# A new written-out order for a fused attention and gated linear unit: other engines for copies, V products and masks, other PSUM banks and buffers

## The chip, the cores and the metric

One core of one Trainium2 chip runs the whole program. The metric is the device time of one execution in microseconds, as the median of several runs. TensorE is called PE in the profile's rows (its weight loads PEld), VectorE DVE, ScalarE ACT, GpSimd POOL and SyncE SP; DMAs here are issued from SP's queue, and two at the start from ACT's.

## The reference, cut to what matters

Eight batches, eight heads, 576 positions, head size 64. A causal attention has a decay bias that depends on running sums of `s`; its output, 512 wide, goes through a gated unit: a causal convolution of 5 taps and a sigmoid make the gate, a matrix product makes the value, a second matrix product the output.

```python
scores = scale * np.matmul(q, k.transpose(0, 1, 3, 2))
cum = np.cumsum(np.maximum(s, 0.0), axis=-1)
bias = -(cum[:, :, :, None] - cum[:, :, None, :])
scores = np.where(causal, -1000000000.0, scores + np.minimum(bias, 0.0))
attn = softmax(scores);  x = heads side by side of np.matmul(attn, v)
gate = 1.0 / (1.0 + np.exp(-sum_k conv_w[k] * shifted(x, 4 - k)))
out = (gate * (x @ w_val)) @ w_out
```

## The kernel before, in words

The work is cut into *pairs*: pair n is two heads of batch n // 4 and also the 128-wide slice n % 4 of that batch's 512 columns. There are 32 of them. The order of all work on all engines is one table of words in the source, `ORDER`. A word such as `vp.1.0:G` or `av0.4:T:6+7` gives a step, its indices, its engine (S SyncE, G GpSimd, T TensorE, A ScalarE, V VectorE) and, after the second colon, the PSUM banks or the buffer that it uses. The program walks the table once and issues each word's instructions on its engine. Each engine then runs its own instructions in that order, and waits by semaphores for what it reads or overwrites. The table is the change; the functions behind the words are the same (line numbers after the change are 3 to 4 lower).

The steps, with the line that the profile shows for them:

- `ld_q`, `ld_k`, `ld_t`, `ld_v`, `ld_s`, `ld_cw`, `ld_wv`, `ld_wo` load (L434, L439, L462, L471, L472, L475 and others), `st` stores (L737); all but two of them stand in SP's queue.
- `c_q`, `c_k` cast queries and keys to bf16 (L377, `qkb<-first`, `qkb<-qkf`); `qt` (batch 0) and `qq` (later batches) transpose them on TensorE (L492, L632); `qe` copies the result from PSUM to `QKT` (L377), for later batches as 512 int32 words, each of which holds two bf16. `tt` and `te` do the same for the last 64 positions (L484).
- `s0`, `s1`, `s2` are the score products of a pair (L508), `e0`, `e1`, `e2` their exponentials into `P` (ScalarE, L559, 1024 columns each). `s4`, `e4` (L535) are the last 64 positions of a batch's four pairs. For pairs 28 to 31 the halves `u0` to `u3` and `f0` to `f3` (L573) take their place.
- The causal mask has two forms. Where the table has a word `mk.n` (or `ml.n`, for the second half of a split pair), GpSimd overwrites with zeros the entries of `P` above the diagonal (L582). Where it has none, two more products on TensorE (`future`, L521) add a large negative number to the scores ahead of the exponential. So a word that is left out of the table puts its mask on TensorE.
- `vp.b.p` is the V product: values of batch b, two heads, times the decay of their key, `Vp <- vst, w` (L478, 128x650, both inputs in SBUF). `av0`, `av` multiply `P` with it (L597), `rec` and `nm` normalise (L610, L616, into `xn`), `xt` transposes (L629), `xe` copies to `xT` (L377; bf16 on VectorE, int32 on ScalarE).
- `t1` is the first two taps of the convolution (VectorE, L671); each of the taps 2 to 4 is either one VectorE instruction that reads PSUM (`t2` to `t4`, L676), or a product `p2` to `p4` into `pr` (GpSimd L660, ScalarE L658) and a sum on GpSimd (L679).
- `th` is the gate's tanh (ScalarE, L696), `val` the value product (L709), `glu` gate times value (VectorE, L718), `out` the output product (L729), `oe` its copy to `ot` (L377).
- `wu` is an unread product: 512 columns of the identity times itself on TensorE, written to a bank and never read (L623).

```python
on_pool = {(f, int(n[0])) for f, *n in (name.split(".") for name, *_ in steps) if f in ("mk", "ml")}
for name, e, *slots in steps:
    ...
    does[f](engines[e], *ix)
```

Of the kernel before, what the change touches and what calls it, by code (L numbers as in the profile page):

```python
# [197 lines left out]
centre:V s0.1:T:4+5:1 ld_k.1.0:S:2 s2.1:T:2+3 e0.1:A qt.0.2.q:T:1 c_k.0.2:V decT:T:0 ld_cw:S e2.0:A qt.0.2.k:T:4
mk.1:G wu.20:T:5 ld_k.1.1:S qe.0.2.k:V wu.21:T:5 wu.22:T:5 qe.0.2.q:A s1.1:T:6+7 c_k.0.3:V e2.1:A s0.2:T:4+5:2
c_q.0.3:G ld_v.0.2:S expw:A qt.0.3.q:T:1 e1.1:A s4.0.1:T:2+3 qe.0.3.q:V vp.0.0:G qt.0.3.k:T:0 qe.0.3.k:V e4.0.1:A  # L200
ld_q.1.0:S:3 e0.2:A s2.2:T:6+7 s1.2:T:2+3 vp.0.1:G av0.0:T:0+1 e2.2:A av.0:T ld_v.0.3:S mk.2:G rec.0:V av0.1:T:4+5
e1.2:A nm.0:V av.1:T c_k.1.0:G:2 s0.3:T:6+7:0 rec.1:V s2.3:T:2+3 e0.3:A nm.1:V ld_t.1:S cwT:T:0 xt.0:T:1 c_k.1.1:G
# [10 lines left out]
ld_v.2.4:S val.3.0:T:4 th.3:A:3 p4.4:G:1 rec.5:V val.3.1:T:1 nm.5:V e1.7:A val.1.0:T:5 glu.3.0:V t4.4:G xt.5:T:2
c_k.2:A:2 glu.3.1:V ld_v.2.1:S val.1.1:T:3 glu.1.0:V s2.7:T:6+7 glu.1.1:V qq.2.0:T:1:5 vp.1.3:G xe.5:V val.0.0:T:3
t2.4:V e2.7:A val.0.1:T:4 t1.5:V:1 p2.5:G:0 qe.2.0:A av0.7:T:6+7 glu.0.0:V glu.0.1:V ld_v.2.3:S val.2.0:T:3 t2.5:G
p3.5:A:1 t3.4:V av.7:T ld_v.2.0:S qe.2.1:A qq.2.1:T:4:2 ld_k.5:S:4 rec.7:V cast_wo:G nm.7:V val.2.1:T:0 qe.2.3:A
xt.6:T:5 glu.2.0:V xt.7:T:1 xe.6:V qe.2.2:A s0.9:T:6+7:1 glu.2.1:V s1.9:T:2+3 p4.5:G:0 xe.7:V out.0.2:T:0 e0.9:A
t1.6:V:0 out.0.0:T:4 t3.5:G t1.7:V:3 e1.9:A ld_k.3:S:0 t4.6:V s1.8:T:6+7 oe.0.2:A:0 s0.8:T:2+3:0 mk.9:G oe.0.0:A:1
t3.7:V val.7.0:T:0 e0.8:A ld_t.4:S out.0.3:T:4 t2.6:V p3.6:G:1 e1.8:A t2.7:V out.0.1:T:2 t3.6:G th.4:A:4 t4.7:V
val.4.0:T:3 st.0.2:S val.7.1:T:7 glu.4.0:V th.7:A:3 val.4.1:T:1 t4.5:G oe.0.3:V:2 th.6:A:1 ld_v.3.2:S s2.8:T:5+6  # L220
glu.7.1:V s4.2.3:T:3+4 glu.7.0:V e2.8:A val.6.0:T:7 glu.4.1:V vp.2.0:G val.6.1:T:0 glu.6.0:V e4.2.3:A ld_v.3.3:S
oe.0.1:V:3 s0.10:T:5+6:2 th.5:A:2 c_q.3:G:0 s2.9:T:3+4 glu.6.1:V av0.8:T:1+2 e2.9:A av.8:T val.5.0:T:0 ld_q.5:S:1
e0.10:A rec.8:V nm.8:V vp.2.1:G s2.10:T:3+4 val.5.1:T:7 e2.10:A glu.5.0:V s1.10:T:1+2 glu.5.1:V s0.11:T:5+6:0 vp.2.2:G
e1.10:A xt.8:T:0 av0.9:T:3+4 xe.8:V tt.3:T:7 e0.11:A p4.8:G:1 t1.8:V:2 av.9:T ld_t.5:S qq.3.0:T:1:2 te.3:A rec.9:V
c_k.3:G:1 nm.9:V s1.11:T:5+6 qe.3.1:A out.0.7:T:7 ld_v.3.4:S t2.8:V qe.3.0:A av0.10:T:3+4 st.0.1:S oe.0.7:V:4 xt.9:T:0
t4.8:G av.10:T e1.11:A xe.9:V ld_v.3.0:S s0.12:T:1+2:1 rec.10:V t1.9:V:3 out.0.6:T:7 e0.12:A vp.2.3:G nm.10:V
ld_v.3.1:S s1.12:T:5+6 oe.0.6:A:5 s2.11:T:1+2 t3.9:V xt.10:T:3 e1.12:A p3.8:G:0 out.0.8:T:7 xe.10:V e2.11:A t4.9:V
ld_q.4:S:2 mk.11:G s2.12:T:5+6 oe.0.8:V:0 e2.12:A qq.3.1:T:4:1 t3.8:G t1.10:V:0 tt.4:T:7 qe.3.3:A av0.11:T:5+6 t2.10:V
st.0.6:S av.11:T p3.10:G:1 qe.3.2:A ld_k.4:S:3 out.0.4:T:1 rec.11:V t4.10:V te.4:A c_q.5:G:2 nm.11:V s0.14:T:3+4:2
st.0.3:S out.0.5:T:7 e0.14:A oe.0.4:V:3 t2.9:V s4.3.3:T:5+6 th.8:A:0 ld_v.4.2:S t3.10:G xt.11:T:4 e4.3.3:A  # L230
s0.13:T:2+3:0 xe.11:V s2.13:T:0+1 e0.13:A ld_v.4.1:S val.8.0:T:5 t1.11:V:1 vp.3.3:G val.10.0:T:6 th.10:A:3 glu.8.0:V
s1.13:T:2+3 t3.11:V vp.3.1:G val.8.1:T:5 e2.13:A st.0.4:S glu.10.0:V t2.11:V e1.13:A val.10.1:T:6 mk.13:G val.9.0:T:0
glu.8.1:V oe.0.5:A:5 ld_k.6:S:0 glu.10.1:V val.9.1:T:1 mk.14:G t4.11:V th.9:A:4 s2.14:T:2+3 qq.5.0:T:7:6 e2.14:A
glu.9.0:V c_k.5:G:0 av0.13:T:4+5 qe.5.0:V av.13:T qe.5.1:A val.11.0:T:0 ld_v.4.4:S rec.13:V glu.9.1:V th.11:A:1
s1.14:T:2+3 s0.15:T:6+7:0 nm.13:V vp.3.2:G e1.14:A val.11.1:T:1 glu.11.0:V xt.13:T:4 ld_v.4.0:S glu.11.1:V e0.15:A
mk.12:G s1.15:T:2+3 xe.13:V s2.15:T:0+1 st.0.5:S t1.13:V:2 e2.15:A qq.5.1:T:7:6 c_q.4:G:1 out.1.1:T:5 t2.13:V qe.5.2:A
qe.5.3:V av0.14:T:0+1 e1.15:A c_k.4:G:2 av.14:T out.1.2:T:7 rec.14:V p4.13:A:0 nm.14:V oe.1.1:A:2 qq.4.0:T:6:2
# [608 lines left out]
```

## Time and profile before

| | |
|---|---|
| three runs | 188.27 us median, 187.43 to 188.32 |
| the profiled execution | 188.6 us, of which the span from first to last instruction is 186.9 us |
| busy share of the span | TensorE 91%, VectorE 86%, ScalarE 86%, GpSimd 88% |
| granted TensorE clock | 0.986 mean |
| HBM traffic | 30.57 MB read, 9.44 MB written |

Busy time on the profile's page is a union: overlapping instructions count once. In the rows of groups the first number after the bar is that busy time, then the mean duration of one; busy time over count is what one more instruction of the kind adds to its engine. Idle time before a group is given with what ended it.

### The profile page before, as it was taken

Reading aid. Unit: us, or ns where it says so; the run is one execution under the profiler, and the core shown is the slowest. Engines: PE = TensorE matmul, PEld = TensorE weight load, DVE = VectorE, ACT = ScalarE, POOL = GpSimd, SP = SyncE. Lnnn points to the kernel's source line nnn. Section 1 sums busy time; section 2 is a strip of 40 time slices with the busy share of each in tenths; the row PEclk is TensorE's granted clock in tenths of the full one; section 3 lists DMA queues with packets and bytes.
Section 4 is the critical chain, followed back from the end, with each engine's and each line's share of the span. In section 5 each row is a group of like instructions: output and inputs, shape, how many; then the busy total and the mean of one; then the engine's idle time right before and its main releaser. Section 6 shows DMA issues by size and latency. Waiting matters only on the chain.

```text
span 186.9 us, 6637 instructions
## 1 busy us (share of the span) xinstructions
PE 170.6 (91%) x2704; PEld 113.4 (61%) x2720; DVE 160.2 (86%) x321; ACT 161.0 (86%) x230; POOL 164.4 (88%) x149
## 2 busy tenths in 40 slices
...
GB/s 173 273 275 300 230 225 255 344 386 328 184 234 329 232 325 276 378 251 278 67 236 182 346 381 270 217 315 267 64 184 44 4 0 117 171 4 56 61 224 175
DMA packets 62283, 40.46 MB, mean 217 GB/s; under 512 B 47333, under 2 KB 49381, under 8 KB 62250
## 3 DMA queue, kind: packets, MB, share of 16 engines
...
HBM read 30.57 MB, written 9.44 MB: 214 GB/s over the span
## 4 chain that ended last, share of the span: by engine, by line
PE 53%; ACT 13%; DMA 8%; SPq 8%; DVE 7%; issue 5%; POOL 3%; ACTq 0%; DVEq 0%; POOLq 0%
PE bank L729 14%; PE bank L709 12%; PE bank L597 11%; PE bank L508 8%; ACT P L559 8%; DMA vst<-in_v_dram 5%; PE bank L629 3%; DMA qkf<-in_k_dram 3%; PE bank L632 3%; SPq L475 3%; ACT th L696 2%; POOL Vp L478 2%; DVE glu L718 2%; DVE gp L676 2%; DVE gp L671 2%
## 5 line engine op out<-in xcount | busy, mean ns | idle before, releaser
L559 ACT ACTIVATE P<-bank 128x1024 bf16<-128x1024 f32 x84 | 82.6, 1032 | 8.5 <-PE bank L508 6.9
L676 DVE SCALAR_TENSOR_TENSOR gp<-bank,cwr,gp 128x574 f32<-128x574 bf16 (+6 forms) x72 | 52.5, 743 | 0.6 <-POOL gp L679 0.2
L679 POOL TENSOR_TENSOR gp<-gp,pr 128x572 f32<-128x572 f32 (+6 forms) x36 | 45.1, 1259 | 5.2 <-DVE gp L676 2.4
L508 PE MATMUL bank<-QKT 64*128 64x128 bf16 (+4 forms) x592 | 38.4, 240 | 4.5 <-ACT P L559 1.7
L478 POOL TENSOR_TENSOR Vp<-vst,w 128x650 bf16<-128x650 f32 x32 | 40.6, 1284 | 1.3 <-ACT w L398 1.1
L709 PE MATMUL bank<-xT,wv 128*128 128x288 bf16 (+2 forms) x256 | 38.5, 287 | 1.0 <-DVE gp L671 0.5
L597 PE MATMUL bank<-Vp,P 128*128 128x65 bf16 x960 | 35.9, 194 | 2.1 <-ACT P L535 0.9
L597 PEld LDWEIGHTS <-P 128*128 128x128 bf16 x960 | 33.1, 98 | 6.2 <-issue 1.3
L729 PE MATMUL bank<-wo,glu 128*128 128x512 bf16 x128 | 34.2, 380 | 1.3 <-issue 0.5
L508 PEld LDWEIGHTS <-QKT 64*128 64x128 bf16 x592 | 19.9, 95 | 22.3 <-issue 15.3
L718 DVE SCALAR_TENSOR_TENSOR glu<-th,bank 128x288 bf16<-128x288 f32 (+2 forms) x64 | 27.6, 446 | 2.3 <-ACT th L696 1.3
L660 POOL TENSOR_TENSOR pr<-xT,cwr 128x572 f32<-128x572 bf16 (+6 forms) x28 | 28.3, 1019 | 1.0 <-DVE xT L377 0.6
L709 PEld LDWEIGHTS <-wv 128*128 128x128 bf16 x256 | 22.4, 97 | 11.0 <-issue 4.7
L616 DVE TENSOR_TENSOR xn<-bank,recs 128x640 bf16<-128x640 f32 (+2 forms) x36 | 26.9, 746 | 0.6
L671 DVE SCALAR_TENSOR_TENSOR gp<-xT,cwr,bank 128x576 f32<-128x576 bf16 (+2 forms) x36 | 26.4, 740 | 0.6
L582 POOL TENSOR_SCALAR_AFFINE_SELECT P<-P 128x1024 bf16<-128x1024 bf16 (+1 forms) x22 | 22.3, 1020 | 4.1 <-ACT P L559 4.1
L696 ACT ACTIVATE th<-gp,cwr 128x576 f32<-128x576 f32 x28 | 21.7, 781 | 0.7 <-DVE gp L676 0.7
L729 PEld LDWEIGHTS <-glu 128*128 128x128 bf16 x144 | 12.3, 98 | 13.1 <-issue 1.7
L377 ACT COPY QKT<-bank 128x512 int32<-128x512 int32 (+1 forms) x26 | 15.3, 625 | 3.8 <-PE bank L492 2.3
L377 ACT COPY ot<-bank 128x512 f32<-128x512 f32 x26 | 15.0, 597 | 1.9 <-PE bank L729 1.1
L629 PE MATMUL bank<-ident,xn 128*128 128x128 bf16 x164 | 15.0, 220 | 0.5 <-ACT P L559 0.3
L610 DVE RECIPROCAL recs<-bank 128x10 f32<-128x10 f32 (+2 forms) x36 | 7.5, 210 | 8.4 <-PE bank L597 7.7
...
## 6 DMA issues: line engine op xcount, KB each, us to landing
...
```

The lines of the kernel that those rows point to most:

```text
L377: (act.copy if e is act else e.tensor_copy)(dst, src)
L478: e.tensor_tensor(Vps[b % 2][:, :, HP[p]], vslot(b)[:, :, HP[p]], w[:, :, b * 8 + 2 * p:b * 8 + 2 * p + 2].unsqueeze(3).to_broadcast([128, ...
L508: pe.matmul(ps[:, hh, c0:c0 + nq], QKTs[b % 2][r, p, k0:k0 + 128, 1], QKTs[b % 2][r, p, q0:q0 + nq, 0], **kw)
L559: act.activation(out=Pt(n)[:, :, step * 512:(step + 1) * 512], in_=pair((f"s{step}", n)), func=AF.Exp, scale=0.125)
L597: pe.matmul(ps[:, o:o + 65], lhsT, Vps[b % 2][:, kb, 2 * p + w, :], start=(kb == 0), stop=(kb == qb))
L660: pool.tensor_tensor(pr, xTs[b % 2][:, c, 4 + lo - m:4 + hi - m], r.to_broadcast([128, hi - lo]), ALU.mult)
L671: vec.scalar_tensor_tensor(gp[:, lo:hi], xT[:, 3 + lo:3 + hi], r, xps(n, *h)[:, lo:hi], ALU.mult, ALU.add)
L676: vec.scalar_tensor_tensor(gp[:, lo:hi], xps(n, *h)[:, lo - m:hi - m], r, gp[:, lo:hi], ALU.mult, ALU.add)
L679: pool.tensor_tensor(gp[:, lo:hi], gp[:, lo:hi], prs[at[f"p{m}", n, *h][0]][:, lo:hi], ALU.add)
L709: pe.matmul(ps, wv[:, dc, c * 128:(c + 1) * 128], xTs[b % 2][:, dc, 4 + lo:4 + hi], start=(dc == 0), stop=(dc == 3))
L718: vec.scalar_tensor_tensor(glu2[:, c, o + lo:o + hi], th[:, lo:hi], 1.0, ps, ALU.add, ALU.mult)
L729: pe.matmul(bank_of(u, i), glu2[:, c, i * 128:i * 128 + 128], wo[:, c, :], start=(c == 0), stop=(c == 3))
```

## The change

The table is written anew: every engine's order, many engines, banks and buffers. Its first lines, and the one function that is shortened because the table no longer gives two banks to one word:

```diff
-ld_k.0.0:A ld_q.0.0:S ld_k.0.1:A wu.0:T:0 ld_t.0:S wu.1:T:7 wu.2:T:0 wu.3:T:7 ld_s:S wu.4:T:0 ld_q.0.1:S wu.5:T:7
+ld_q.0.0:S ld_k.0.0:A ld_s:S ld_k.0.1:A ld_t.0:S ld_k.0.2:S c_q.0.0:V ld_cw:S qt.0.0.q:T:0 c_k.0.0:A ld_q.0.1:S relu:V
...
     def val_part(n, hf):
-        two = at["val", n, 0][0]
-        j = two[hf] if isinstance(two, list) else at["val", n, hf][0]
+        j = at["val", n, hf][0]
```

What the words add up to:

| steps | before | after |
|---|---|---|
| V products | 32 GpSimd | 21 GpSimd, 11 VectorE |
| masks on GpSimd | 18 whole, 4 of a half | 14 whole |
| masks on TensorE | 10 whole, 4 of a first half | 14 whole, 4 of a first half, 4 of a second half |
| taps 2 to 4 on VectorE | 72 | 63 |
| tap sums on GpSimd | 36 | 45 |
| tap products | 28 GpSimd, 8 ScalarE | 32 GpSimd, 13 ScalarE |
| `qe` copies | 26 ScalarE, 10 VectorE | 17 ScalarE, 19 VectorE |
| `xe` copies | 12 ScalarE, 24 VectorE | 22 ScalarE, 14 VectorE |
| `te` copies | 6 ScalarE, 2 VectorE | 7 ScalarE, 1 VectorE |
| unread products | 32, all before pair 4's first `av0` | 14: 11 before that, 3 after the last output product |

One whole cast of queries (`c_q.3`) goes from GpSimd to VectorE, and `c_k.0.0` from VectorE to ScalarE. The loads of batches 0 and 1 keep their count in SP's queue: the last V load of batch 1 is its 37th in both.

Three places, as the engines' own sequences. First GpSimd at the V products of batch 1 (`Vp_110`; `P` are exponentials to be masked, `gp` tap sums, `pr` tap products). Before:

```order
L582 AFFINE_SELECT P_118<-P_118 128x2x512
L679 TENSOR_TENSOR gp_120<-gp_120,pr_134 128x574
L478 TENSOR_TENSOR Vp_110<-vst_93,w 128x5x130
L582 AFFINE_SELECT P_116<-P_116 128x2x512
L478 TENSOR_TENSOR Vp_110<-vst_93,w 128x5x130 x2
L377 CAST wv<-qkf_138 128x2048
```

After:

```order
L676 TENSOR_TENSOR gp_120<-gp_120,pr_134 128x572
L475 TENSOR_TENSOR Vp_110<-vst_93,w 128x5x130
L676 TENSOR_TENSOR gp_120<-gp_120,pr_135 128x573
L657 TENSOR_TENSOR pr_134<-xT_113,cwr 128x572
L374 CAST wv<-qkf_138 128x2048
```

Of the three V products that GpSimd made here one is left, and the masks between them are gone. VectorE at the same place, after the change (before, no V product stood on VectorE anywhere):

```order
L668 SCALAR_TENSOR_TENSOR gp_122<-xT_113,cwr,bank 128x576
L673 SCALAR_TENSOR_TENSOR gp_121<-bank,cwr,gp_121 128x572
L673 SCALAR_TENSOR_TENSOR gp_122<-bank,cwr,gp_122 128x573
L475 TENSOR_TENSOR Vp_110<-vst_93,w 128x5x130 x2
L673 SCALAR_TENSOR_TENSOR gp_122<-bank,cwr,gp_122 128x574
```

Two of batch 1's V products now stand between taps on VectorE, ahead of tap 2 of pair 3, and what comes after that tap is the first normalisation of batch 1.

Last, ScalarE where batch 4's queries and keys are copied from PSUM (`QKT_107`), at 88 to 95 us of the trace before; `CAST QKT_108` is `te.5`, the copy of batch 5's tail. Before:

```order
L658 ACTIVATE pr_134<-bank,cwr 128x572
L377 COPY ot_130<-bank 128x512
L377 COPY QKT_107<-bank 128x2x256
L377 COPY xT_114<-bank 128x288
L377 COPY QKT_107<-bank 128x2x256 x2
L377 COPY ot_133<-bank 128x512
L377 CAST QKT_108<-bank 128x4x128
```

After:

```order
L655 ACTIVATE pr_135<-bank,cwr 128x574
L374 COPY ot_130<-bank 128x512
L655 ACTIVATE pr_134<-bank,cwr 128x572
L374 COPY QKT_107<-bank 128x2x256
L374 COPY xT_114<-bank 128x288
L374 COPY QKT_107<-bank 128x2x256
L655 ACTIVATE pr_135<-bank,cwr 128x573
L374 CAST QKT_108<-bank 128x4x128
```

One `QKT` copy and an `ot` copy have left this stretch, and two tap products have come in.

More of the change, by code (lines that the diff above doesn't have):

```diff
@@ L198 @@
[L198 to L202, printed above, removed]
@@ L213 @@
[L213 to L217, printed above, removed]
@@ L218 @@
[L218 to L237, printed above, removed]
@@ new lines @@
+ld_v.2.2:S glu.1.1:V xt.5:T:3 c_k.2:A:2 qe.2.0:V val.1.0:T:1 t4.4:G av0.7:T:5+6 glu.1.0:V av.7:T xe.5:V xt.6:T:7
+glu.3.1:V t3.4:G val.2.1:T:1 qe.2.1:A rec.7:V t1.5:V:2 val.2.0:T:0 xe.6:A p3.5:A:1 nm.7:V val.0.1:T:2 cast_wo:G p3.6:A:0
+ld_v.2.1:S qq.2.1:T:4:3 glu.2.0:V glu.2.1:V s0.9:T:5+6:2 qe.2.3:A glu.0.1:V xt.7:T:0 t1.6:V:0 e0.9:A s1.9:T:1+2 t3.5:G
+out.0.0:T:3 t2.6:V xe.7:A ld_v.2.0:S e1.9:A out.0.2:T:5 t4.6:V p4.5:G:1 ld_v.2.4:S qe.2.2:A t1.7:V:3 s1.8:T:1+2
+s0.8:T:6+7:0 oe.0.0:A:0 ld_q.3:S:3 t3.6:G oe.0.2:V:1 th.4:A:4 val.4.0:T:4 t3.7:V out.0.1:T:3 e0.8:A p2.5:G:0 t2.7:V
@@ new lines @@
+val.4.1:T:5 e1.8:A val.6.0:T:6 t4.7:V ld_t.3:S t4.5:G out.0.3:T:7 th.6:A:0 oe.0.1:V:2 th.7:A:3 glu.4.1:V ld_k.3:S:4
+s2.8:T:0+1 t2.5:G s4.2.3:T:2+3 glu.4.0:V val.7.1:T:5 glu.6.0:V e4.2.3:A oe.0.3:V:4 val.7.0:T:4 e2.8:A ld_v.3.4:S
+val.6.1:T:6 vp.2.0:G glu.7.1:V glu.7.0:V st.0.3:S s2.9:T:2+3 th.5:A:1 glu.6.1:V ld_v.3.2:S s2.10:T:0+1 s0.10:T:4+5:1
+c_q.3:V:0 vp.2.1:G e2.9:A av0.8:T:6+7 av.8:T e0.10:A val.5.0:T:2 vp.2.3:G rec.8:V val.5.1:T:3 nm.8:V e2.10:A
+s0.11:T:4+5:0 st.0.0:S glu.5.0:V s1.10:T:6+7 glu.5.1:V c_k.3:G:1 ld_t.4:S e0.11:A xt.8:T:0 vp.2.2:V av0.9:T:1+2 tt.3:T:3
@@ new lines @@
+val.12.1:T:0 e0.18:A glu.14.0:V xt.16:T:1 vp.4.1:G oe.1.3:V:2 s1.18:T:5+6 xe.16:A s2.18:T:3+4 glu.12.1:V e1.18:A
+val.13.1:T:7 ld_v.5.3:S t2.15:V vp.4.2:G val.12.0:T:0 e2.18:A glu.13.1:V s4.5.3:T:5+6 t1.16:V:1 val.15.1:T:2 mk.18:G
+e4.5.3:A val.13.0:T:7 t3.16:V th.15:A:3 s0.19:T:3+4:1 c_k.6:G:0 glu.13.0:V val.15.0:T:5 e0.19:A glu.12.0:V av0.18:T:6+7
+glu.15.1:V av.18:T glu.15.0:V ld_v.5.4:S s1.19:T:2+3 c_q.6:G:2 rec.18:V s2.19:T:4+5 ld_v.5.1:S nm.18:V e1.19:A
+out.1.4:T:0 t2.16:V e2.19:A xt.18:T:6 s0.20:T:2+3:2 xe.18:V p4.16:G:1 qq.6.1:T:1:7 oe.1.4:A:0 t1.18:V:3 ld_v.5.0:S
```

152 lines of the change are left out of this document (82 added, 70 removed).

## The prediction

> **What bounds the kernel now.** I read the busy shares first, then the chain of work that ended last, then the engines by stretch. The page's first lines, and three stretches (length, then busy us of PE, PEld, DVE, ACT, POOL, granted clock, DMA share, GB/s) with a fourth that stands out:
>
> ```profile
> PE 170.6 (91%) x2704; PEld 113.4 (61%) x2720; DVE 160.2 (86%) x321; ACT 161.0 (86%) x230; POOL 164.4 (88%) x149
> PE 53%; ACT 13%; DMA 8%; SPq 8%; DVE 7%; issue 5%; POOL 3%; ACTq 0%; DVEq 0%; POOLq 0%
> 0.00:40.00 40.00, 32.93 (x501) 20.41 (x502) 28.40 (x57) 31.73 (x43) 31.88 (x38) 0.96 0.99 268
> 40.00:180.00 140.00, 134.81 (x2192) 91.81 (x2206) 130.13 (x256) 126.95 (x184) 132.53 (x112) 1.00 0.73 202
> 180.00:187.00 7.00, 2.81 (x16) 1.20 (x14) 1.64 (x9) 2.28 (x5) 0.00 (x0) 0.86 0.57 208
> 90.00:100.00 10.00, 7.95 (x143) 5.67 (x141) 8.75 (x15) 7.43 (x13) 8.51 (x8) 1.00 0.70 169
> ```
>
> All four compute engines are nearly full, and over half of the chain is TensorE. From 40 to 180 us TensorE stands idle 5.2 us, 2.05 of them between 90 and 100; VectorE has 9.9 us free there, ScalarE 13.0, GpSimd 7.5. Before 40 us nobody is full and DMA is busy throughout (0.99). So an engine may get some work in the middle for nothing, TensorE hardly any; and a better order can win at most what TensorE waits.
>
> **The change part by part.** The prices, as busy time over count of these groups:
>
> ```profile
> L676 DVE SCALAR_TENSOR_TENSOR gp<-bank,cwr,gp 128x574 f32<-128x574 bf16 (+6 forms) x72 | 52.5, 743 | 0.6 <-POOL gp L679 0.2
> L679 POOL TENSOR_TENSOR gp<-gp,pr 128x572 f32<-128x572 f32 (+6 forms) x36 | 45.1, 1259 | 5.2 <-DVE gp L676 2.4
> L660 POOL TENSOR_TENSOR pr<-xT,cwr 128x572 f32<-128x572 bf16 (+6 forms) x28 | 28.3, 1019 | 1.0 <-DVE xT L377 0.6
> L658 ACT ACTIVATE pr<-bank,cwr 128x572 f32<-128x572 bf16 x4 | 3.0, 755 | 0.1
> L478 POOL TENSOR_TENSOR Vp<-vst,w 128x650 bf16<-128x650 f32 x32 | 40.6, 1284 | 1.3 <-ACT w L398 1.1 <-DMA out_dram<-ot 0.2
> L616 DVE TENSOR_TENSOR xn<-bank,recs 128x640 bf16<-128x640 f32 x28 | 23.0, 821 | 0.6
> L582 POOL TENSOR_SCALAR_AFFINE_SELECT P<-P 128x1024 bf16<-128x1024 bf16 x18 | 20.6, 1152 | 4.1 <-ACT P L559 4.1
> L582 POOL TENSOR_SCALAR_AFFINE_SELECT P<-P 128x256 bf16<-128x256 bf16 x4 | 1.7, 426 | 0.0
> L377 ACT COPY QKT<-bank 128x512 int32<-128x512 int32 x22 | 12.5, 604 | 1.5 <-PE bank L632 1.3
> L377 DVE COPY QKT<-bank 128x512 int32<-128x512 int32 x6 | 4.1, 684 | 0.0
> L377 DVE COPY xT<-bank 128x576 bf16<-128x576 bf16 x21 | 9.5, 452 | 1.2 <-PE bank L629 0.9 <-ACT th L696 0.2
> L377 ACT COPY xT<-bank 128x288 int32<-128x288 int32 x7 | 2.8, 406 | 0.3 <-PE bank L629 0.2
> L377 POOL CAST qkb<-qkf 128x2048 bf16<-128x2048 f32 x6 | 11.3, 1898 | 0.0
> L623 PE MATMUL bank<-ident 128*128 128x512 bf16 x32 | 10.9, 460 | 1.4 <-POOL ident masks.py:199 1.4
> L521 PE MATMUL bank<-fut,fut 64*128 64x512 bf16 x20 | 4.1, 398 | 0.0
> L521 PE MATMUL bank<-fut,fut 64*128 64x256 bf16 x14 | 1.9, 269 | 0.0
> ```
>
> No V product ran on VectorE. Its nearest row is `xn`, also a two-input product with a broadcast operand and nearly as many columns: 0.82 us. Half of that to GpSimd's own 1.27 us bound it; I take 0.8.
>
> - GpSimd: 11 V products off (−14.0), 4 whole and 4 half masks off (−4.6, −1.7), one cast off (−1.9), 9 tap sums on (+11.3), 4 tap products on (+4.0): −6.9 us.
> - VectorE: 11 V products on (+8.8), 9 taps off (−6.6), 9 `qe` on (+6.2), 10 `xe` off (−4.5), a tail copy off (−0.7), casts +1.2 (the 2048-wide one as four of the 0.41 us casts below, one small one off): +4.4 us.
> - ScalarE: 9 `qe` off (−5.1), 10 `xe` on (+4.0), 5 tap products on (+3.4, one of them narrow), a tail copy and a small cast on (+1.2, as two `QKT` copies): +3.5 us.
> - TensorE: 18 unread products off (−6.1). Four more whole masks are eight products of 0.205 us (+1.6), four half masks eight of 128 columns, some 0.11 us by the 256-wide row's 0.136 (+0.9).
>
> These are loads, not time. What reaches the end:
>
> *The front, to 40 us.* Up to pair 5's second exponential ScalarE has, counted word by word, a tap product, two `QKT` copies and a tail copy less (0.75 + 1.15 + 0.6) and a small cast and three `xT` copies more (0.6 + 1.2): −0.7 us. Its exponentials wait 3.0 us for scores before 40 us, some of it beside unread products (who waited for whom, us, times, longest; then start, length, instruction):
>
> ```profile
> ACT P L559 <- PE bank L508: 3.0, 5, 0.8
> ...
> 33.23 2.06 PE L623 MATMUL bank<-ident 128*128 128x512 bf16 x5
> 33.40 1.94 ACT L559 ACTIVATE P<-bank 128x1024 bf16<-128x1024 f32 x2 [0.76 <-PE bank L508]
> 35.66 0.60 ACT L535 ACTIVATE P<-bank 128x512 bf16<-128x512 f32 x1 [0.33 <-PE bank L521]
> 5.71 0.81 PE L623 MATMUL bank<-ident 128*128 128x512 bf16 x3
> 28.00:36.00 8.00, 6.53 (x86) 2.93 (x83) 7.79 (x11) 6.91 (x9) 8.00 (x8) 0.79 1.04 284
> 26.82 4.58 DMA vst<-in_v_dram
> ```
>
> I credit 0.8 us of them: front −1.5 us. More is excluded by the last row: batch 1's last values land at 31.4 us, the 37th issue of SP's queue before and after; what gains there is that two engines share the V products behind that landing.
>
> Five unread products took 0.41 us each at 33.2 us, where the granted clock of the stretch is 0.79; three at 5.7 us took 0.27. With 7 instead of 23 unread products up to the third exponential of pair 3, TensorE may run slowly for longer. Bounds: nothing, or twice the time for the useful products of the first 15 us, of which ScalarE would feel perhaps 1.5 us. I take +0.3, near the lower end, since ScalarE's queue is dense there. [...]
>
> *The middle.* The gap at 90 to 100 us is a ring of waits: TensorE waits for a copy on ScalarE, then ScalarE for the tail's transposes behind it:
>
> ```profile
> 92.41 1.54 PE L597 MATMUL bank<-Vp,P 128*128 128x65 bf16 x45 [0.87 <-ACT ot L377]
> 94.46 0.58 ACT L377 CAST QKT<-bank 128x512 bf16<-128x512 f32 x1 [2.33 <-PE bank L484]
> ```
>
> There the new order takes a `QKT` and an `ot` copy off ScalarE. Between nothing and all 5.2 us of TensorE's idle time can go; no row says how much, so I take half, −2.6 us. Masks stand against it: of the whole ones the front gets three more on TensorE, the rest of the run one, and the half ones are all in the last 30 us, where TensorE is full: +0.4 +0.9 = +1.3 us.
>
> *VectorE against GpSimd.* The row that speaks against this change:
>
> ```profile
> 8.23 1.35 DVE L386 TENSOR_TENSOR_SCAN gp<-gp 64x576 f32<-64x576 f32 x1
> 8.39 2.08 POOL L582 TENSOR_SCALAR_AFFINE_SELECT P<-P 128x1024 bf16<-128x1024 bf16 x1 [2.37 <-ACT P L559]
> 12.81 1.09 POOL L582 TENSOR_SCALAR_AFFINE_SELECT P<-P 128x1024 bf16<-128x1024 bf16 x1 [1.77 <-ACT P L559]
> 11.71 0.41 DVE L377 CAST qkb<-first 128x512 bf16<-128x512 f32 x1
> 13.85 0.61 POOL L377 CAST qkb<-first 128x512 bf16<-128x512 f32 x1
> 13.91 0.83 DVE L377 CAST qkb<-first 128x512 bf16<-128x512 f32 x1
> ```
>
> A mask of 1.09 us took 2.08 beside a scan whose inputs are both in SBUF, and a VectorE cast of 0.41 us took 0.83 beside a GpSimd cast. The moved V products have two SBUF inputs, and GpSimd is nearly always busy. If each waits for the rest of GpSimd's instruction, half of 1.28 us on the mean, VectorE pays 11 × 0.64 = 7.0 us more, and GpSimd 11 × 0.8 = 8.8, more than the 6.9 it was given. VectorE's free time absorbs part; bounds on the path are 0 and 7.0, I take a tenth, +0.7, as the waits are spread over eight batches and VectorE heads 7% of the chain. [...]
>
> The cover for ScalarE's +3.5 us is its 13.0 free us of the middle. If that is gone, the exponentials are late, then `av`.
>
> *Sum*: −1.5 + 0.3 − 2.6 + 1.3 + 0.7 = −1.8 us. The profiled execution, 188.6 us (span 186.9 and 1.7 around it), gives 186.8; the median of the runs is 0.3 lower: 186.5 us.
>
> **The rivals.** (a) The port. VectorE would be the fullest engine with 160.2 + 4.4 + 7.0 = 171.6 us, and GpSimd at 164.4 − 6.9 + 8.8 = 166.3 would stand beside TensorE's 167.0; `rec`, `nm` and `glu` queue behind each waiting V product, and TensorE waits for them. With half of the 7.0 us on the path, 186.5 + 2.8 = 189.3 us. From a third of the 7.0 us on, the change is slower than before. For it: the rows above; against: 9.9 us of free time. (b) The order is only another order: the middle's waits go to other places, and −2.6 becomes about −0.8: 188.3 us, no change. For it: 53% of the chain is TensorE, whose work outside the front does not shrink. (c) Nearly all of TensorE's idle time goes, −4.7 instead of −2.6: 184.4 us. For it: VectorE and ScalarE have 9.9 and 13.0 us to spare there; against: a ring of waits needs every engine on time, and the free time is being spent. (d) The slow clock in front costs 1.5 us, and the new order gains only as in (b): 189.5 us. For it: 0.79 beside a thin stretch.
>
> **How the numbers follow.** Forecast 40%, (c) 10%, (b) 25%, (a) 18%, (d) 7%. About 0.5%, 0.9 us, is what a measurement tells from no change: faster 0.50, same 0.25, slower 0.25. The range from 183.9 to 189.8 us reaches to (c) and (a); the forecast's own is 185.4 to 187.3.
>
> **What would show it.** Right: ScalarE passes pair 5's second exponential before 39.5 us; no 2 us hole in TensorE's row near 90 us; V products on VectorE with a mean over 1 us, some up to 2, and GpSimd rows stretched beside them. Wrong: VectorE at 97% from 40 to 180 us with TensorE waiting for `xn` or `glu` (a); TensorE's idle time there still 5 us (b) or under 1 (c); granted clock under 0.9 in the first stretches (d).

## The result and the profile after

The change made the kernel slower: 200.47 us in the median of four runs (199.94 to 201.47) against 188.30 for the order before; ratio 1.066, with a 95% interval of 1.0604 to 1.0715. The forecast was 186.5 us with a range to 189.8. Ratios compare fast executions alone, while medians take all; in run 7 below one execution of four took 268.1 us, and in run 5 one took 535.8.

The profiled execution took 200.5 us (span 198.8). Its page, then three stretches in the same columns as the prediction's (length, busy us of PE, PEld, DVE, ACT, POOL, granted clock, DMA share, GB/s):

```profile
PE 170.4 (86%) x2718; PEld 112.7 (57%) x2718; DVE 176.3 (89%) x321; ACT 164.5 (83%) x238; POOL 168.5 (85%) x142
DVE 43%; PE 37%; issue 9%; ACT 5%; DMA 3%; POOL 1%; DVEq 0%; SPq 0%; ACTq 0%
```

```profile
0.00:40.00 40.00, 27.44 (x483) 18.45 (x483) 31.25 (x57) 30.71 (x42) 31.19 (x36) 1.00 1.01 275
40.00:180.00 140.00, 128.38 (x2116) 86.20 (x2113) 131.94 (x228) 122.41 (x172) 129.65 (x97) 0.99 0.68 191
90.00:100.00 10.00, 7.83 (x183) 5.51 (x182) 9.23 (x15) 8.15 (x14) 8.93 (x7) 1.00 0.43 98
```

VectorE has gained 16.1 us of busy time where the loads said 4.4, and it now heads the chain (7% before, 43% after). From 40 to 180 us TensorE stands idle 11.6 us instead of 5.2; a hole of the same size is still there at 90 to 100 us (2.17 us, before 2.05).

The groups that tell why VectorE is fuller, first VectorE's, then GpSimd's:

```profile
L475 DVE TENSOR_TENSOR Vp<-vst,w 128x650 bf16<-128x650 f32 x11 | 17.8, 1624 | 0.0
L374 DVE CAST qkb<-qkf 128x2048 bf16<-128x2048 f32 x1 | 2.2, 2159 | 0.0
L742 DVE TENSOR_SCALAR ok<-okt 128x20 bf16<-128x20 f32 x1 | 1.3, 1322 | 0.0
L741 DVE TENSOR_TENSOR okt<-cwr 128x20 f32<-128x20 f32 x1 | 1.3, 1305 | 0.0
...
L475 POOL TENSOR_TENSOR Vp<-vst,w 128x650 bf16<-128x650 f32 x21 | 28.8, 1386 | 1.0 <-ACT w L395 0.7 <-DMA vst<-in_v_dram 0.3
L579 POOL TENSOR_SCALAR_AFFINE_SELECT P<-P 128x1024 bf16<-128x1024 bf16 x14 | 17.2, 1237 | 0.6 <-ACT P L556 0.6
```

A V product on VectorE takes 1.62 us on the mean, twice the 0.8 that the prediction took for one without a wait. On GpSimd the V products and masks are longer too (1386 and 1237 ns, before 1284 and 1152). One place, VectorE first, then GpSimd (start, length, instruction):

```profile
63.44 2.04 DVE L475 TENSOR_TENSOR Vp<-vst,w 128x650 bf16<-128x650 f32 x1
65.39 0.45 DVE L374 COPY xT<-bank 128x576 bf16<-128x576 bf16 x1
...
62.90 1.89 POOL L374 CAST qkb<-qkf 128x2048 bf16<-128x2048 f32 x1
64.74 1.69 POOL L579 TENSOR_SCALAR_AFFINE_SELECT P<-P 128x1024 bf16<-128x1024 bf16 x1
```

The V product starts inside GpSimd's cast and ends 0.7 us after the cast does, about its own length. GpSimd's mask, which follows the cast, is in turn 0.6 us longer than its usual 1.1. Each waits for the other once. "The port", in the prediction and below, is a name for this waiting; the traces show the waits, not what lies behind them. All eleven V products on VectorE ended 0.69 to 0.70 us behind the end of the GpSimd instruction that was running when they began, and GpSimd's next instruction was 0.5 to 0.6 us longer than others of its form.

Second, the tail. Again VectorE, then GpSimd:

```profile
159.72 0.81 DVE L673 SCALAR_TENSOR_TENSOR gp<-bank,cwr,gp 128x574 f32<-128x574 bf16 x1
162.04 1.53 DVE L673 SCALAR_TENSOR_TENSOR gp<-bank,cwr,gp 128x573 f32<-128x573 bf16 x2 [1.51 <-POOL gp L676]
...
167.00 1.30 DVE L741 TENSOR_TENSOR okt<-cwr 128x20 f32<-128x20 f32 x1
168.34 1.32 DVE L742 TENSOR_SCALAR ok<-okt 128x20 bf16<-128x20 f32 x1
...
160.61 2.75 POOL L676 TENSOR_TENSOR gp<-gp,pr 128x572 f32<-128x572 f32 x2 [1.39 <-DVE gp L673]
```

At 160 us a GpSimd sum of pair 24 stands between two VectorE taps of the same pair, so each engine waits for the other. At 167 us two instructions of 20 columns (the check of the taps, `chk0`) take 2.6 us instead of the 0.6 that they took before, and the scores of the last pairs wait for the `glu` behind them. Three of the waits of the new order from 154 to 180 us:

```profile
PE bank L725 <- DVE gp L673: 1.9, 2, 1.6
DVE gp L673 <- POOL gp L676: 1.5, 1, 1.5
PE bank L505 <- DVE glu L714: 1.4, 1, 1.4
```

Step by step along the same instructions in both traces, the new order is 3.3 us late with its first exponential (10.56 us instead of 7.30), level again at 39 us (+0.2), some 3 late at 70 us, 4.4 at 150 us (pair 27's second exponential), and 12.0 at the last copy. So 4.2 us are lost in the middle and 7.6 behind that.

### The profile page after: what moved, and what is told of

Its sections match the earlier page's. It is cut to its first block, busy times and chain, and to the rows that moved or that the text cites. A ratio compares the mean times of both kernels' runs of the same rounds, so it can differ in the third digit from the quotient of the medians.

```text
span 198.8 us, 6677 instructions
## 1 busy us (share of the span) xinstructions
PE 170.4 (86%) x2718; PEld 112.7 (57%) x2718; DVE 176.3 (89%) x321; ACT 164.5 (83%) x238; POOL 168.5 (85%) x142
## 4 chain that ended last, share of the span: by engine, by line
DVE 43%; PE 37%; issue 9%; ACT 5%; DMA 3%; POOL 1%; DVEq 0%; SPq 0%; ACTq 0%
DVE gp L673 11%; PE bank L705 9%; PE bank L594 7%; DVE gp L668 7%; PE bank L725 7%; PE bank L505 6%; DVE xn L613 5%; DVE glu L714 5%; DVE Vp L475 4%; DVE QKT L374 4%; PE bank L626 3%; DMA gp<-in_s_dram 3%; DVE xT L374 2%; ACT pr L655 2%; ACT P L556 2%
## 5 line engine op out<-in xcount | busy, mean ns | idle before, releaser
L676 POOL TENSOR_TENSOR gp<-gp,pr 128x572 f32<-128x572 f32 (+6 forms) x45 | 60.4, 1345 | 11.7 <-DVE gp L673 6.5
L673 DVE SCALAR_TENSOR_TENSOR gp<-bank,cwr,gp 128x574 f32<-128x574 bf16 (+6 forms) x63 | 46.0, 734 | 4.2 <-POOL gp L676 1.9
L505 PE MATMUL bank<-QKT 64*128 64x128 bf16 (+4 forms) x592 | 39.7, 241 | 7.3 <-DVE QKT L374 1.8
L705 PE MATMUL bank<-xT,wv 128*128 128x288 bf16 (+2 forms) x256 | 39.2, 290 | 1.5 <-DVE glu L714 0.7
L725 PE MATMUL bank<-wo,glu 128*128 128x512 bf16 x144 | 36.3, 380 | 4.6 <-DVE gp L673 2.2
L594 PEld LDWEIGHTS <-P 128*128 128x128 bf16 x960 | 33.2, 98 | 7.6 <-issue 1.7
L657 POOL TENSOR_TENSOR pr<-xT,cwr 128x572 f32<-128x572 bf16 (+6 forms) x32 | 34.1, 1071 | 2.5 <-ACT xT L374 1.4
L475 POOL TENSOR_TENSOR Vp<-vst,w 128x650 bf16<-128x650 f32 x21 | 28.8, 1386 | 1.0 <-ACT w L395 0.7
L475 DVE TENSOR_TENSOR Vp<-vst,w 128x650 bf16<-128x650 f32 x11 | 17.8, 1624 | 0.0
L579 POOL TENSOR_SCALAR_AFFINE_SELECT P<-P 128x1024 bf16<-128x1024 bf16 x14 | 17.2, 1237 | 0.6 <-ACT P L556 0.6
L570 ACT ACTIVATE P<-bank 128x768 bf16<-128x768 f32 x16 | 12.4, 812 | 4.8 <-PE bank L518 2.4
```

Source lines behind the costliest of these rows:

```text
L475: e.tensor_tensor(Vps[b % 2][:, :, HP[p]], vslot(b)[:, :, HP[p]], w[:, :, b * 8 + 2 * p:b * 8 + 2 * p + 2].unsqueeze(3).to_broadcast([128, ...
L505: pe.matmul(ps[:, hh, c0:c0 + nq], QKTs[b % 2][r, p, k0:k0 + 128, 1], QKTs[b % 2][r, p, q0:q0 + nq, 0], **kw)
L594: pe.matmul(ps[:, o:o + 65], lhsT, Vps[b % 2][:, kb, 2 * p + w, :], start=(kb == 0), stop=(kb == qb))
L657: pool.tensor_tensor(pr, xTs[b % 2][:, c, 4 + lo - m:4 + hi - m], r.to_broadcast([128, hi - lo]), ALU.mult)
L673: vec.scalar_tensor_tensor(gp[:, lo:hi], xps(n, *h)[:, lo - m:hi - m], r, gp[:, lo:hi], ALU.mult, ALU.add)
L676: pool.tensor_tensor(gp[:, lo:hi], gp[:, lo:hi], prs[at[f"p{m}", n, *h][0]][:, lo:hi], ALU.add)
```

## The experiments

"Before" is the old order, run again on the same chip each time (187.7 to 188.9 us). Edits are to the table unless code is shown. The ratios are to it, with 95% intervals. A trace is of one execution; "late" and "ahead" compare the start of the same instruction with the trace before the change.

**The V products and the check, undone.**

```diff
-vp.0.2:V ... vp.7.1:V      (11 words)      # run 1: back on GpSimd, same places
+vp.0.2:G ... vp.7.1:G
-        e.tensor_tensor(okt, rf, rf, ALU.mult)                # run 2: out of check0, into
-        e.tensor_scalar(ok[:, 4:24], okt, 1e12, None, ALU.is_le)    # conv_ratio, near 24 us
-c_q.3:V:0                                   # run 3: runs 1 and 2 together, and
+c_q.3:G:0                                   # this cast back on GpSimd
```

Run 1:

> The new order with its 11 V products of VectorE back on GpSimd, each at its own place in the table. Theory 1 (the port): the 12.2 us that the change cost come mainly from two-input VectorE instructions that wait for GpSimd's instruction in progress, and from GpSimd's next one, stretched in turn. VectorE's busy time falls from 176.3 to about 158.5 us (17.8 off); GpSimd does 14 us more of V products and loses some 11 us of stretching, so it ends at 170 to 173; the time falls to 189 to 194 us, and GpSimd rows show their old durations (tap sums 1.26 busy over count, masks 1.1). Theory 2 (the order): the banks, buffers and the order of the other steps cost it, and the V products' place does not matter: 198 to 203 us, GpSimd being fuller.

Run 2:

> The new order with only the two small instructions of the check (20 columns: the square of the taps, the comparison) moved from 167 us to the computation of the tap ratios, near 24 us; the two reductions stay. Theory 1 (the port): in the result they took 1.30 and 1.32 us instead of 0.39 and 0.18 because GpSimd was at work, and TensorE waited for glu behind them: the time falls by 1.5 to 2.6 us, to 198 to 199. Theory 2 (the order): VectorE waits there for something else in the tail: the time falls by less than 0.5 us.

Run 3:

> The new order with the 11 V products and the cast of batch 3's queries back on GpSimd, and the check's two small instructions moved to the tap ratios. Theory 1 (the port): 187 to 191 us, as no VectorE instruction after 45 us reads two SBUF inputs. Theory 2 (the order): 197 us or more, with GpSimd over 172 us busy. In between, by how far it stays above 188.3, the rest is the order's.

Measured: 204.5 us (ratio 1.0894, 1.0826 to 1.0962), 200.2 us (1.0658, 1.0606 to 1.0709) and 204.6 us (1.0862, 1.0813 to 1.0911). Theory 1, as I had stated it, fell: with the V products back the kernel is 4 us slower still, not faster. Runs 2 and 3 lie where theory 2 had them, run 1 above both. The page of run 1 points at GpSimd:

```profile
PE 172.1 (85%) x2718; PEld 114.2 (57%) x2718; DVE 160.3 (80%) x310; ACT 164.0 (81%) x238; POOL 175.2 (87%) x153
```

VectorE is as free as before the change, and GpSimd, which keeps the 9 more tap sums, carries 175 us; ScalarE's tanh waits 8.5 us for GpSimd's sums, where it waited 0.8 in the change. As it stands, the new plan cannot take the V products back.

In run 2 the time is 0.3 us lower, which is within the scatter, but its trace shows two effects that cancel. At their new place, too, the check's two instructions run beside GpSimd, and each ends within 0.03 us of GpSimd's instruction of the time (a product of 16 columns just ahead of them takes 0.17 us):

```profile
22.46 0.63 DVE L412 TENSOR_TENSOR okt<-cwr 128x20 f32<-128x20 f32 x1
23.12 1.07 DVE L413 TENSOR_SCALAR ok<-okt 128x20 bf16<-128x20 f32 x1
```

The normalisation behind them starts 1.85 us later than in the change, and the exponentials stay 1.8 us later up to 90 us and are 2.7 later at pair 28. Behind that, run 2 is 3.4 us faster than the change. So the check's waits did cost time in the tail; the new place took it back.

**One factor in the old order.**

```diff
-vp.0.2:G ... vp.7.1:G      (the same 11 words, old table)
+vp.0.2:V ... vp.7.1:V
```

Run 4:

> The order before the change with one thing changed: the same 11 V products on VectorE instead of GpSimd, each at its old place in the table. Theory 1 (the port): VectorE gets 11 x 0.8 = 8.8 us of work and as much in waits (1.6 us each on the mean, up to 2.2), on top of 160.2; GpSimd gets 14 us less and its neighbours are stretched by 0.7 to 1.0 us each: 192 to 199 us. Theory 2 (the order): VectorE's 9.9 free us of the middle take the V products, GpSimd is relieved: 186 to 190 us, and they take 0.8 to 1.0 us each.

Measured: 196.8 us, ratio 1.0483 (1.0424 to 1.0541): 8.8 us slower, in theory 1's range. These V products alone, in the old order, cost 8.8 us where the whole change cost 12.2. They take 1.26 us on the mean, less than expected; the three during which GpSimd ran nothing took 0.83. But this adds work to VectorE as well as waits. To part them:

**The same V products without the second SBUF operand** (in the new order, and in the old one with them on VectorE). `vbank` names for each a bank that was written some words ago.

```diff
-    w[:, :, b * 8 + 2 * p:b * 8 + 2 * p + 2].unsqueeze(3).to_broadcast(...), ALU.mult
+    bank[:, vbank[b, p], 0:10].rearrange("p (i h) -> p i h", h=2).unsqueeze(3).to_broadcast(...), ALU.not_equal
```

Run 7:

> The new order, in which VectorE's 11 V products take their second input from a PSUM bank (ten columns of a bank that at that point in the table was written some words ago and is written again some words later) instead of the decay in SBUF, and compare instead of multiply, so that the values stay finite. It leaves out the decay of those heads. Place, engine, columns and output stay. Theory 1 (the port): with one SBUF input they no longer wait for GpSimd and take 0.8 to 0.95 us instead of 1.62, and GpSimd's casts and sums beside them are not stretched (V products on GpSimd back to 1.28 us): the time falls to 190 to 194 us. Theory 2 (the order): they get shorter, but the end stays at 197 us or more, other waits taking their place.

Run 8:

> The order before the change with the same 11 V products on VectorE as in the fourth run (196.8 us), but with the second input from a PSUM bank as in the run above. Same order, same engines, same load for VectorE; only where the second operand lies differs. Theory 1 (the port): nearly all of the 8.8 us that the fourth run lost come back: 187 to 190 us, V products 0.8 to 0.95 us. If it is VectorE's load (11 x 0.8 = 8.8 us more work) or the place in its queue that cost them: 194 us or more.

Measured: new order 195.2 us (1.0361, 1.0308 to 1.0413; 194.6 without the execution of 268.1), old order 194.3 (1.0296, 1.0226 to 1.0366). VectorE's V products of the run in the old order with two SBUF operands, of the one with a PSUM operand there, and of the new order with a PSUM operand, the last (run 7) with GpSimd's V products and masks:

```profile
L477 DVE TENSOR_TENSOR Vp<-vst,w 128x650 bf16<-128x650 f32 x11 | 13.9, 1260 | 0.1
```

```profile
L480 DVE TENSOR_TENSOR Vp<-vst,bank 128x650 bf16<-128x650 f32 x11 | 9.1, 824 | 1.2 <-ACT P L565 1.1
```

```profile
L479 DVE TENSOR_TENSOR Vp<-vst,bank 128x650 bf16<-128x650 f32 x11 | 9.0, 822 | 1.6 <-PE bank L513 1.0 <-ACT P L564 0.3 <-ACT pr L663 0.2
L483 POOL TENSOR_TENSOR Vp<-vst,w 128x650 bf16<-128x650 f32 x21 | 27.8, 1340 | 1.0 <-ACT w L396 0.7 <-DMA vst<-in_v_dram 0.3
L587 POOL TENSOR_SCALAR_AFFINE_SELECT P<-P 128x1024 bf16<-128x1024 bf16 x14 | 15.2, 1095 | 0.7 <-ACT P L564 0.6
```

With one SBUF operand they take 0.82 us, and GpSimd's masks fall from 1237 to 1095 ns. In the new order this is worth 5.3 us (5.8 without that execution): the port's price. Its trace, of an execution of 192.9 us, is 1.4 us *ahead* of the old order at the first half exponential of pair 28 and loses 5.6 behind it, which points to a fault of the tail's own. In the old order only 2.5 of the 8.8 us come back: the forecast for the port alone, 187 to 190 us, missed, and 194.3 is where load or place had been put. The bank reads bring waits there too: the run with them is 1.7 us behind the one without at 50 us. Behind 50 us the traces lose 6.1 us with the port and 3.0 without. These 3.0 are not the second SBUF operand's; that they are VectorE's work in places planned for GpSimd is likely, not shown.

**All engine choices, all order.** The new table with every engine of the old one, and the reverse. Words for masks and tap products that the other table has are put in or taken out; 12 and 6 words move ahead of their bank's next use.

Run 5:

> The new order with every step on the engine that it had before the change: all V products on GpSimd, 18 whole and 4 half masks on GpSimd, 9 taps and the products behind them as before, the copies and casts as before. Words that the new table lacks stand right behind the exponential (masks) or some words ahead of their tap (products); 12 steps stand a few words earlier so that they read their bank before it is written again. Theory 1 (engines: port and load): 188 to 193 us, as in the table before. Theory 2 (the order itself, with its banks and buffers): 198 us or more.

Run 6:

> The order before the change with every step on the engine that the change gives it (11 V products and one cast of 2048 columns on VectorE, 14 masks on GpSimd, 9 more tap sums there, the copies); 6 steps stand a few words earlier so that they read their bank before it is written again. Theory 1 (engines): 197 to 202 us, at least the 8.8 us that the V products alone cost in this order. Theory 2 (the order): 188 to 193 us, because the other engine choices relieve what the V products cost.

Measured: 232.2 us (1.2325) and 227.2 us (1.1989). Both are far above anything that either theory had a reason for, so the pair doesn't tell them apart. Either order with the other's engines loses some 40 us. It suggests that an order and its engine choices are one plan, though the words put in and moved have a share in the loss that nothing here separates.

**The tail, changed for the old one.** Cut where both tables have the same steps behind them; the rest in the other's order, banks and engines.

Run 9:

> The new order up to and with the third exponential of pair 27 (about 152 us in its trace), then the remaining steps in the order, on the engines and in the banks and buffers of the table before. Theory A (the tail has a fault of its own): what the new order lost behind that point, 7.5 us in the trace of the result and 5.6 in the run whose V products read a PSUM operand, comes back: 193 to 195.5 us. Theory B (the loss is made earlier, by the V products that wait for GpSimd, and the tail only arrives late): 198 to 201 us.

Run 10:

> The reverse: the order before the change up to and with the third exponential of pair 27, then the remaining steps as in the new order. No V product stands on VectorE but those that the new tail holds, which is none. Theory A (a fault of the tail): 188.3 and 4 to 7.5 us more: 192 to 196 us. Theory B: 187.5 to 189.5 us.

Run 11:

> The first of these with VectorE's 11 V products reading a PSUM bank as their second operand and comparing instead of multiplying (it leaves out the decay of those heads). If the port of the V products and the tail are the two causes, both are away, and what is left is what the rest of the new order brings: the trace of the run with the PSUM operand was 1.4 us ahead of the order before at pair 28: 186 to 188 us, the gain that the prediction had forecast. If a third cause exists: over 189.5 us.

Measured: 197.2 us (1.0476, 1.0384 to 1.0568), 196.4 (1.0393, 1.0290 to 1.0497) and 191.3 (1.0141, 1.0056 to 1.0225). The stretch from 154 to 180 us of the old order, the new one, the old head with the new tail, the new head with the old tail, and the same with the PSUM operand:

```profile
154.00:180.00 26.00, 25.79 (x326) 17.10 (x328) 25.34 (x65) 23.48 (x44) 22.04 (x28) 1.00 0.25 89
```

```profile
154.00:180.00 26.00, 22.41 (x296) 14.68 (x295) 22.29 (x46) 19.71 (x32) 20.35 (x19) 0.93 0.17 62
```

```profile
154.00:180.00 26.00, 22.61 (x285) 14.32 (x287) 22.80 (x50) 19.75 (x32) 17.87 (x17) 0.93 0.15 53
```

```profile
154.00:180.00 26.00, 23.51 (x308) 15.33 (x305) 23.97 (x53) 22.25 (x37) 25.34 (x26) 1.00 0.17 63
```

```profile
154.00:180.00 26.00, 25.02 (x317) 15.93 (x318) 25.39 (x61) 22.52 (x40) 23.77 (x28) 1.00 0.20 73
```

With the new tail TensorE idles 3.4 to 3.6 us here whatever came before; with the old one 0.2 and 1.0, and 2.5 in run 9, of which 2.3 lie ahead of pair 28. Run 9 fell between the two ranges and run 10 0.4 us above theory A's, but the traces bear theory A out. Run 10 is on time at pair 27's second exponential (0.1 us late) and 8.2 late at the last copy, with no V product on VectorE. Run 9 is 8.2 us late at pair 28's first half exponential, 2.8 of them lost since pair 27's second exponential, where the tables are joined, and 8.1 at the last copy: the old tail loses nothing. In time, the tail is worth 3.3 us behind the new head (200.5 to 197.2), 3.9 without the port (195.2 to 191.3), and costs 8.6 behind the old head (7.4 by the ratio). Run 11 says that a third cause exists: 3.5 us above the old order remain.

**Two places of the tail mended** (with the PSUM operand; the check early as in run 2):

```diff
-... t2.24:V t4.24:G t3.24:V ...   t3.30.1:G ... t2.30.1:V   t4.29.1:G ... t2.29.1:V
+... t2.24:V t3.24:V t4.24:G ...   t2.30.1:V t3.30.1:G ...   t2.29.1:V t4.29.1:G ...
```

Run 12:

> The new order with the PSUM operand (195.2 us), and in its tail two places mended: the check's two small instructions stand at the tap ratios instead of 160 us, and in pairs 24, 29 and 30 (second halves) a VectorE tap that stood behind a GpSimd sum of the same pair now stands ahead of it. It leaves out the decay of the 11 V products. If these two places are the tail's fault (VectorE waited 1.5 us for the sum and 2.0 us for GpSimd's port): 191 to 192.5 us. If the waits only go to the next step of the same rings: within 1 us of 195.2.

Measured: 193.2 us (1.0268, 1.0178 to 1.0357), 2.0 less than run 7 with intervals that overlap, and short of the forecast. Behind pair 28's first half exponential its trace loses 3.6 us instead of run 7's 5.6, but it comes there 2.0 later, 0.7 of them lost at the check's new place. Among its waits from 154 to 166 us:

```profile
POOL gp L687 <- DVE gp L684: 2.3, 1, 2.3
ACT th L704 <- POOL gp L687: 1.5, 1, 1.5
PE bank L516 <- ACT ot L375: 1.3, 1, 1.3
```

VectorE no longer waits for GpSimd there, but GpSimd's sum waits for the second tap, the tanh on ScalarE waits for it, an output copy stands behind the tanh, and TensorE waits 1.3 us for that copy's bank. The wait went round the ring: this tail needs another order, not one swap.

**The prediction's terms by themselves**: the old table without its four `ml` words; the old table without the 18 unread products; the new table with `s0.0` ahead of `qt.0.1.k`, `tt.0` and three unread products.

Run 13:

> The order before the change with one thing changed: the four masks of the second halves (pairs 28 to 31) on TensorE instead of GpSimd, as the change has them. The prediction's price: 8 products of 128 columns on a full TensorE, +0.9 us: 189 us or a little more. If GpSimd's relief (1.7 us less work in the last 30 us) is worth as much or more: 187.5 to 188.3 us.

Run 14:

> The order before the change without the 18 unread products that the change leaves out; nothing else moves. The prediction's price: -0.8 us for waits beside them and +0.3 for a slower clock: 187.5 to 188.5 us. If TensorE's clock needs them (the slow clock rival): 189 to 190 us, with a granted clock below 0.9 in the first stretches or matmuls that take twice as long there. If the front's end is set by the loads of batch 1 alone, no change: 188.0 to 188.5.

Run 15:

> The new order with the first scores of pair 0 ahead of the transposes of keys of pair 1, of the tail's and of three unread products, behind which they stand on TensorE (one unread product writes bank 5 instead of 3). In the result the first exponential began 3.3 us later than before, and nothing of it was left at 39 us. If the front's loss is made up at the loads: 200 to 200.8 us as in the result, and the first exponential at 7 to 7.5 us. If it is carried through in another form: 197 to 198.5 us.

Measured: 188.5 us (ratio 0.9991, 0.9952 to 1.0030), 190.3 us (1.0071, 1.0029 to 1.0113) and 203.1 us (1.0735, 1.0686 to 1.0784). The half masks on TensorE show no cost. Leaving out the unread products does: 0.7%, and pair 5's second exponential is 2.2 us late. Without them the same products on TensorE are slower (old order first, then without):

```profile
10.20 1.03 PE L623 MATMUL bank<-ident 128*128 128x512 bf16 x4
11.27 0.63 PE L508 MATMUL bank<-QKT 64*128 64x128 bf16 x12
11.83 0.40 PE L492 MATMUL bank<-ident,qkb 128*128 128x128 bf16 x4
```

```profile
12.08 1.03 PE L506 MATMUL bank<-QKT 64*128 64x128 bf16 x12 [0.47 <-DVE chalf L387]
13.05 0.61 PE L490 MATMUL bank<-ident,qkb 128*128 128x128 bf16 x4
```

Twelve score products take 1.03 instead of 0.63 us and four transposes 0.61 instead of 0.40. The granted clock from 10 to 20 us reads 1.00 in both traces, so it does not show why. Run 15 missed both its forecasts, 2.7 us above the change. Its first exponential came at 7.86 us instead of 10.56, but the next one waited 3.1 us for scores, and pair 5's second exponential came 1.7 us later than in the change: putting one step first moved the wait and lost more than it gained.

**The true decay through PSUM, with the old tail.** TensorE copies ten columns of the decay into columns 490 to 509 of a bank that holds another step's result (`wp`, ten words); the V product reads them there. Then one store moved ahead in SyncE's queue; then two more moves.

```diff
+    def decay(e, b, p):
+        pe.matmul(bank[:, at["wp", b, p][0], 490 + p % 2 * 10:500 + p % 2 * 10]..., identf,
+                  w[:, :, b * 8 + 2 * p:b * 8 + 2 * p + 2], start=True, stop=True)
...
-ld_v.5.0:S st.0.8:S ld_q.7:S:1 st.1.1:S ld_v.6.1:S      # second kernel: st.1.1 behind st.0.4
+st.0.4:S st.1.1:S ld_v.4.4:S ...
```

Run 16:

> The new order with the old tail, in which ten of VectorE's 11 V products read their true decay from free columns of a PSUM bank, where TensorE has put it by one small product each (ten columns of the decay, by the identity in fp32); the first, of batch 0, still reads SBUF. All work is done. If the port is what the run with the PSUM operand took away: V products of 0.82 us, and 191.3 us of that run with this tail plus at most 1 us for ten small products: 191 to 192.5 us. If the comparison in place of the product or the missing wait for the decay was what helped: 195 us or more, near the 197.2 of the new order with the old tail.

Run 17:

> The run before (decay from PSUM, old tail, 192.6 us) with one word moved: the store of output block 1 of the second half of batches stands 150 words earlier in SyncE's queue, right behind an older store, instead of behind the loads of batch 5's values and batch 7's queries. If this store is what VectorE's copy into the same buffer waited for at 121.7 us (1.3 us, and TensorE 1.3 us behind it): 190.5 to 191.3 us, and no wait of that copy for a store. If the loads that now come later take it back: 192 to 193 us.

Run 18:

> The same, and two more: the new order is kept up to the second exponential of pair 27 (13 words more, so the seam lies behind batch 6's attention), and the V product of batch 2 that stood ahead of a copy of xT stands behind that pair's first tap. If what is left of the loss are these places: 188.5 to 190.5 us. If the rest is spread over the whole order: 191 us or more.

Measured: 192.6 us (1.0188, 1.0142 to 1.0234), 191.6 (1.0165, 1.0114 to 1.0216) and 192.3 (1.0182, 1.0133 to 1.0232). The first shows the port with nothing left out of the work: it is 4.6 us below run 9 (197.2), which has the same order without the ten words, though the ten words add work. Its V products, without and with the second SBUF operand:

```profile
L483 DVE TENSOR_TENSOR Vp<-vst,bank 128x650 bf16<-128x650 f32 x10 | 8.2, 828 | 1.1 <-ACT P L568 0.4 <-DMA vst<-in_v_dram 0.2 <-DMA tail<-in_k_dram 0.2
L487 DVE TENSOR_TENSOR Vp<-vst,w 128x650 bf16<-128x650 f32 x1 | 1.1, 1086 | 0.0
```

The store's run is 0.9 us faster than this, between its two forecasts and with intervals that overlap: a gain is not shown. From 114 to 130 us, the waits that the store caused, and what stands there when it is moved:

```profile
PE bank L717 <- DVE ot L377: 1.3, 1, 1.3
DVE ot L377 <- DMA out_dram<-ot: 1.3, 1, 1.3
```

```profile
POOL Vp L486 <- DMA vst<-in_v_dram: 1.2, 1, 1.2
DVE Vp L482 <- DMA vst<-in_v_dram: 0.5, 1, 0.5
```

The copy no longer waits; the V products now wait for the loads that the store was moved ahead of. The two further moves gained nothing. No version of the new order came under the old one: the best that does all the work, 191.6 us, stands 1.1 to 2.2% above it.

## Why the prediction was wrong, point by point

- *The port, +0.7.* This is the step that failed most. It had the right row and the right mechanism, and it even worked out the 7.0 us on VectorE; the trace shows 8.8 (11 × 0.80). What failed is the share: I put a tenth on the path, because 9.9 us were free and VectorE headed 7% of the chain. Measured on the path are 5.3 us (run 7; 4.6 with all work done, run 16), 0.6 of the waits. What stands behind a V product on VectorE comes late, as rival (a) said: from 40 to 152 us TensorE waits 1.5 us for `xn`, 1.0 for a tap, 0.7 for `glu` and 0.7 for a `QKT` copy. 10 of the 11 V products took longer than 0.82 us, from 1.10 to 2.23. With all 7.0 us on the path instead of 0.7 the sum would have come to 192.8 us (186.5 + 6.3), nearer to the result than 186.5 or rival (a)'s 189.3, but partly by luck, as it has nothing of the tail in it. I also counted only V products: the cast of 2048 columns (2.16 us), and the check's two small instructions (2.6 instead of 0.6), had no term.
- *The tail: no term at all.* The sum had the front, the middle and the masks, and the last 40 us only as "half masks, +0.9". They lost 7.6 us in the trace of the result, and run 10 shows 7.4 to 8.6 us for the tail alone. The old tail was full (TensorE 25.79 of 26 us): a full stretch can only be kept or lost, and a new order there needed an adverse bound.
- *The middle, −2.6.* Without the port the trace gains 0.4 us between 39 us and pair 28 (0.98 ahead, then 1.39; 1.94 ahead at pair 27's second exponential), not 2.2 (−2.6, and +0.4 for whole masks). That is nearer to rival (b), whose −0.8 had the waits go to other places. TensorE's idle time from 40 to 150 us, 4.9 us before, is 8.0 after and 4.2 with the PSUM operand; the hole at 90 us kept its size. But it is another hole: before, TensorE waited there for ScalarE's copy (0.87 us), and now for VectorE, which had taken over `QKT` copies and V products (a tap 1.0 us, a `QKT` copy 0.7). So the ring that I read was opened, and the wait moved to the engine that got the work. Half of the idle time was a guess without a row.
- *The front, −1.5 and +0.3.* My sign for it was badly set: pair 5's second exponential runs from 38.9 to 39.9 us, and ran from 38.7 to 39.7 before the change, so "before 39.5" cannot tell the two by the start and fails by the end. The front gained nothing; it is 0.2 us late. Without the port the trace is 1.0 us ahead there, near the −1.2. But the first exponential came 3.3 us late, which I had not read from the order. The clock's term was too small where it could be tested: in the old order the missing unread products cost 1.3 us net, nearly rival (d)'s 1.5, and the 0.8 that I credited for them did not show. Its upper bound, twice the time, had no figure beside it: the trace before has products of 512 columns at 0.41 us (unread, at 33.2 us) and at 0.205 (of a mask), and in run 14 scores and transposes took 1.5 to 1.6 times as long at 12 to 14 us, where the granted clock read 1.00.
- *Masks, +1.3.* The +0.9 for the half masks came out as −0.2 us (−0.9 to +0.6). GpSimd's relief of 1.7 us in the same stretch may be the reason; that was not tested.
- *The loads.* VectorE +4.4 was right (with the waits 16.1 measured; 4.4 + 8.8 + 2.0 + 0.5 is 15.7), ScalarE +3.5 was right, and 0.8 for a V product was right (0.82). GpSimd came out 4.1 us fuller (168.5) instead of 6.9 emptier; with the PSUM operand it is 161.9. But "free" time did not take work: in the old order the V products without the port still cost 5.9 us, the bank reads' waits included.
- Rival (a) named the port and put 189.3 on it; no rival had the tail, and none added the two.

What stays open: of the 12.2 us, about 5.3 are the port's and about 3.9 the tail's; some 3 us above the old order remain with both away. In run 11's trace they arise late in the head: it is 1.4 us ahead at 121 us, 1.2 late at 129, 3.1 late at pair 28 and no later at the end. The seam of the joined tables, the store and the bank reads are in them, and single traces differ there by up to 2 us, so they are not parted. The 9 more tap sums on GpSimd, the whole masks and the moved copies had no run of their own.
